# Turning q and k of the last twelve sets by transposing DMA transfers, with scores in tiles of 64 rows and a new order of all engines

## The chip, the core and the metric

The kernel runs on one core of one Trainium2 chip. The metric is device time in microseconds, the median over the executions shown. The engines are TensorE (PE, with its weight loads as PEld), VectorE (DVE), ScalarE (ACT), GpSimd (POOL) and SyncE (SP). PE writes to PSUM, of which the kernel uses eight banks of 128 x 512 f32. DMAs issued by POOL go through queue 0, which can cast f32 to f16 on the way; those issued by SP and ACT go through the hardware queues 1 and 10. All use the core's 16 DMA engines.

## The reference

An attention over 8 batches x 8 heads, 576 tokens, head dimension 64, with 16 "beacon" keys and values ahead of the causal ones, then a two-layer feed-forward net over all 4608 tokens:

```python
k_all = np.concatenate([beacon_k, k], axis=2)          # [8, 8, 592, 64]
v_all = np.concatenate([beacon_v, v], axis=2)
scores = scale * np.matmul(q, k_all.transpose(0, 1, 3, 2))
causal[:, Nb:] = np.triu(np.ones((S, S), dtype=bool), k=1)
scores = np.where(causal, -1000000000.0, scores)
a = np.exp(scores - scores.max(-1, keepdims=True))
a /= a.sum(-1, keepdims=True) + 1e-09
x = (a @ v_all)                                        # [4608, 512] after putting the heads side by side
h = x @ w_in                                           # w_in [512, 2048]
g = h * (1.0 / (1.0 + np.exp(-1.702 * h)))
out = g @ w_out                                        # w_out [2048, 512], out f32
```

## The kernel before

The attention is cut into 16 *sets*: set s is batch s // 2 and four of its eight heads. The work on a set:

- `load_qk` / `e_load_qk` (line 416): POOL issues one casting DMA each for q and k. In the tiles `qn` and `kn` (three buffers each) a head has 32 partitions, and a partition holds a run of 18 tokens (2304 bytes in f16).
- `turns` / `e_turn` (lines 457, 465, 472): DVE casts the beacon keys and turns them, then k and q, by 32x32 transposes on pairs of f16 seen as one f32. In `kT` and `qT` (two buffers each) a head has 32 partitions, one for each pair of its 64 dimensions; the two halves of the pair, d = 0 and 1, lie side by side.
- `chunk` / `e_qk` (line 506): PE makes the scores, keys on partitions, queries on columns. The 1664 columns that the causal mask leaves of a set are cut into chunks of 512 (sets 0 to 3 by a cut of their own); a chunk from set 4 on may end one set and begin the next. Each piece of a chunk is eight matmuls in tiles of 32 rows: for d = 0 and 1, four heads at once, accumulated in PSUM. There are 39 such chunks for sets 4 to 15.
- `e_exp` (line 518) on ACT takes the chunk from PSUM to `E`; `e_mask` (line 536) on POOL zeroes the triangles on the diagonal; DVE adds up key blocks for the sum (`e_zadd`, line 554).
- `e_av` (line 594): PE multiplies `E` by v and by ones, in tiles of 32 columns; DVE turns, inverts and turns the sums (lines 604, 610, 615) and writes the normalised result into `xT` (`e_norm`, line 628), a ring of 2304 token columns.

The feed-forward net works on ten groups of tokens (two of 256, eight of 512). Groups 0 and 1 use plain products (`e_m1`, line 652, and `e_m2`, line 698); groups 2 to 9 make the second product by seven half-size products with sums of blocks (`products`, `e_s` at line 718, `e_prod` at line 770, `e_join` at line 786). Groups 7, 8 and 9 (`FAST`) make the first product that way too (`fast`, `e_part`, line 864), with the sums of weights kept in the buffers of `qn`, `kn` and `bkf` once the sets are done with them.

Nothing is scheduled at run time: `ORDER` at the top is a list of operation numbers for each engine, and `Plan.run` merges the lists into the order in which the program is written, by costs of its own, and hands out PSUM banks: four that any tile of the net and of `e_av` can take, four for scores until the last chunk's exps are done. POOL's DMA issues stand in POOL's list between the masks; the stores, and the small beacon loads, stand in SP's.

PE changes its tile mode between 32-row scores, 32-column value products and full matmuls.

## Time and profile before

| what | us |
|---|---|
| median of 2 runs (320.57 and 320.72) | 320.64 |
| span of the profiled execution | 319.1 |
| PE busy | 312.4 (98%) |
| PE weight loads busy | 223.9 (70%) |
| DVE busy | 246.5 (77%) |
| ACT busy | 220.0 (69%) |
| POOL busy | 113.2 (35%) |
| packets of queue 0, share of 16 DMA engines' span | 49.0% |

The span runs from the first to the last instruction of the profiled execution; the 1.5 us to the median lie around it, and no time of its own is given for that execution besides. Busy times are unions, so a busy PE says that some matmul is in flight and not that the array is filled at its peak. In a line of a view, `out<-in` names what is written and read, with buffer numbers left out; `L506` is line 506 of the kernel before. A wait is put down to what ended it.

### The profile page before, as it was taken

How to read it: one execution, taken by the hardware profiler on the slowest of the kernel's cores; microseconds unless marked ns; L12 is line 12 of the kernel's file. 1: busy time of each engine (PE TensorE's matmuls, PEld its weight loads, DVE VectorE, ACT ScalarE, POOL GpSimd, SP SyncE). 2: the span in 40 equal slices, each digit the busy share in tenths (PEclk: the TensorE clock that was granted, in tenths of full speed). 3: DMA queues.
4: the chain of work that ended last, by engine and by line, in shares of the span. 5: the costliest groups of instructions: out<-in, count | busy, mean ns of one | idle time of the engine just before them, and what ended most of it. 6: DMA issues, size and time to landing. Idle time of an engine off the chain costs nothing.

```text
span 319.1 us, 9554 instructions
## 1 busy us (share of the span) xinstructions
PE 312.4 (98%) x4119; PEld 223.9 (70%) x4119; DVE 246.5 (77%) x484; ACT 220.0 (69%) x275; POOL 113.2 (35%) x178
## 2 busy tenths in 40 slices
PE   6999999999999999999999999999999999999995
PEld 2567855544875467754778877646788888888884
DVE  4769966896797778875788979888978975684773
ACT  1777986557767686698867685778779786666520
POOL 8768488670238413472084108420420000000000
PEclk9999999999999999999999999999999999999999
DMA  7999999993109911398085707710021000011112
GB/s 122 175 202 209 206 192 185 170 228 65 37 2 165 208 26 37 46 153 123 7 81 90 115 2 81 100 35 2 2 83 51 4 20 15 33 69 36 67 68 99
DMA packets 58379, 28.80 MB, mean 90 GB/s; under 512 B 41312, under 2 KB 53728, under 8 KB 58336
## 3 DMA queue, kind: packets, MB, share of 16 engines
q0 software_dynamic: 47552, 18.49, 49.0%
q1 hardware_dynamic: 10576, 9.63, 9.3%
q8 instruction: 32, 0.52, 0.7%
q14 instruction: 11, 0.09, 0.1%
q10 hardware_dynamic: 208, 0.07, 0.1%
HBM read 37.22 MB, written 9.44 MB: 146 GB/s over the span
## 4 chain that ended last, share of the span: by engine, by line
PE 89%; DMA 5%; POOL 2%; ACT 1%; DVE 1%; issue 0%; DVEq 0%; POOLq 0%
PE u L770 31%; PE u L652 25%; PE u L864 12%; PE u L594 9%; PE s L506 8%; PE u L698 5%; DMA kn<-in_k_dram 3%; DMA qn<-in_q_dram 2%; POOL w L438 1%; ACT E L518 1%; ACT L674 0%; DVE kT L472 0%; POOL qn L416 0%; POOL kn L416 0%; ACT g L674 0%
## 5 line engine op out<-in xcount | busy, mean ns | idle before, releaser
L518 ACT ACTIVATE E<-s 128x2048 f16<-128x2048 f32 (+3 forms) x59 | 90.7, 1552 | 35.4 <-PE s L506 32.5
L652 PE MATMUL u<-xT,w 128*128 128x256 f16 (+1 forms) x512 | 87.9, 326 | 0.1
L536 POOL TENSOR_SCALAR_AFFINE_SELECT E<-E 128x512 f16<-128x512 f16 (+3 forms) x78 | 48.7, 643 | 89.6 <-ACT E L518 89.5
L652 PEld LDWEIGHTS <-w 128*128 128x128 f16 x512 | 49.2, 98 | 32.8 <-issue 1.1
L674 ACT ACTIVATE g<-u 128x512 f16<-128x512 f32 x80 | 43.6, 598 | 15.9 <-PE u L652 15.6
L770 PEld LDWEIGHTS <-g 128*128 128x128 f16 x512 | 48.4, 98 | 7.6 <-issue 0.5
L786 DVE SCALAR_TENSOR_TENSOR osb<-u,osb 128x512 f32<-128x512 f32 (+2 forms) x51 | 33.2, 654 | 21.5 <-PE u L770 16.3
L770 PE MATMUL u<-w,g 128*128 128x256 f16 x384 | 49.7, 273 | 0.0
L770 PEld LDWEIGHTS <-sA 128*128 128x128 f16 x384 | 36.6, 98 | 6.0 <-issue 0.8
L892 ACT ACTIVATE g<-u 128x512 f16<-128x512 f32 x48 | 27.2, 602 | 14.0 <-PE u L864 8.6
L506 PEld LDWEIGHTS <-kT 32*128 32x128 f16 x1088 | 22.4, 92 | 17.5 <-issue 10.8
L770 PE MATMUL u<-tB,sA 128*128 128x256 f16 x256 | 34.2, 273 | 0.0
L628 DVE TENSOR_TENSOR xT<-u,rz 128x352 f16<-128x352 f32 (+2 forms) x52 | 26.1, 521 | 8.4 <-PE u L594 7.7
L506 PE MATMUL s<-qT,kT 32*128 32x192 f16 (+14 forms) x992 | 30.9, 247 | 0.5 <-ACT E L518 0.3
L432 POOL DMA_DIRECT2D vb<-in_v_dram x32 | 27.8, 873 | 3.1 <-PE u L594 1.4
L594 PE MATMUL u<-E,vb 128*32 128x352 f16 (+8 forms) x928 | 27.7, 262 | 0.1
L594 PEld LDWEIGHTS <-vb 128*32 128x32 f16 (+1 forms) x928 | 20.1, 96 | 6.7 <-issue 2.9
L554 DVE TENSOR_TENSOR zs<-zs,E 128x1344 f16<-128x1344 f16 (+2 forms) x36 | 21.8, 605 | 0.9
L472 DVE STREAM_TRANSPOSE kT<-kn 128x576 f32<-128x576 f32 x16 | 20.1, 1256 | 2.7 <-DMA kn<-in_k_dram 2.2
L718 DVE TENSOR_TENSOR sA<-g 128x512 f16<-128x512 f16 x32 | 13.2, 417 | 10.9 <-ACT g L674 10.7
L472 DVE STREAM_TRANSPOSE qT<-qn 128x576 f32<-128x576 f32 x16 | 19.8, 1240 | 0.8 <-DMA qn<-in_q_dram 0.7
L864 PEld LDWEIGHTS <-w 128*128 128x128 f16 x192 | 18.7, 98 | 2.3
(76 smaller groups left out, 401.1 us busy)
## 6 DMA issues: line engine op xcount, KB each, us to landing
out_dram<-osb SPq DMA_DIRECT2D x35, 256.0 KB, 2.6
kn<-in_k_dram POOLq DMA_DIRECT2D x16, 288.0 KB, 6.8
qn<-in_q_dram POOLq DMA_DIRECT2D x16, 288.0 KB, 6.4
vb<-in_v_dram POOLq DMA_DIRECT2D x24, 128.0 KB, 6.8
w<-in_moe_w_in_dram POOLq DMA_DIRECT2D x8, 256.0 KB, 9.4
w<-in_moe_w_out_dram POOLq DMA_DIRECT2D x4, 512.0 KB, 12.1
vb<-in_v_dram POOLq DMA_DIRECT2D x8, 112.0 KB, 6.0
vb<-in_v_dram POOLq DMA_DIRECT2D x8, 80.0 KB, 6.8
```

What stands on the lines that cost most here:

```text
L432: nc.gpsimd.dma_start(out=t[0 : hi - lo, j, h0:h1, :], in_=v[b, h0:h1, lo:hi, :].rearrange("h n d -> n h d"),)
L472: nc.vector.transpose(out=f32(dst.rearrange("p n e -> p (n e)")).rearrange("p (r t) -> p t r", t=TR), in_=f32(src[:, :]).rearrange("p (t c ...
L506: nc.tensor.matmul(u[:, o : o + w], kT[s % NB2][r : r + 32, j * P : (j + 1) * P, d], qT[s % NB2][r : r + 32, a : a + w, d], start=(d == 0) ...
L518: nc.scalar.activation(out=Es[s][:, h0:h1, c0:c1], in_=sall[(i, p)][:, :, o : o + c1 - c0], func=AFT.Exp, scale=0.125,)
L536: nc.gpsimd.affine_select(out=blk, in_=blk, compare_op=ALU.is_ge, fill=0.0, base=off + (Nb if j == 0 else 0), pattern=[[0, Q], [1, w]], ch ...
L594: nc.tensor.matmul(u[32 * h : 32 * h + 32, a:e], lhs, src[0:kw, h, col : col + e - a], start=first, stop=last, skip_group_check=s >= EARLY ...
L652: nc.tensor.matmul(u[:, o + a - t0 : o + e - t0], w1t[:, kp, nt * P : (nt + 1) * P], xT[:, kp, a % XR : (e - 1) % XR + 1], start=(kp == 0 ...
L674: nc.scalar.activation(out=gts[g][:, n0:n1, 0:w], in_=rings[("m1", g, n0)][:, 0 : n * w].rearrange("p (n w) -> p n w", n=n), func=AFT.Gelu ...
L770: nc.tensor.matmul(u[:, HM * mt : HM * (mt + 1)], lhs[:, n, mt * P : (mt + 1) * P], rhs[:, n, :], start=(n == 0 and (mt == 0 or apart) and ...
L786: nc.vector.scalar_tensor_tensor(out=osbs[(g, dst)][:, c0:c1], in0=rings[("p", g, p)][:, c0:c1], scalar=scale_of(g), in1=osbs[(g, src)][:, ...
L864: nc.tensor.matmul(u[:, HM * n : HM * (n + 1)], lhs[x][:, (2 * i + n) * P : (2 * i + n + 1) * P], rhs[:, x, :], start=fresh and n == 0 and ...
L892: nc.scalar.activation(out=gts[g][:, n : n + 2, HM * h : HM * (h + 1)], in_=rings[src][:, :].rearrange("p (n w) -> p n w", n=2), func=AFT. ...
```

## The change

- Sets 0 to 3 are turned as before, from two buffers instead of three. For sets 4 to 15, q and k of a whole batch (two sets) are first loaded into `qS` and `kS`, tokens on partitions and all eight heads side by side: per batch five loads of q, five of k and one of the beacon keys, all issued by POOL (`e_stage`). `qS` and `kS` have one buffer each, whose memory is also that of the early sets' `qn` and `kn`; the loads of a batch wait until the batch before it is turned.
- SP then issues ten transposing DMAs a set (`e_xbar`), five for k and five for q, each of up to 128 tokens x 256 columns (four heads), into the memory of `kT` and `qT`, now seen as `kP` and `qP`: two heads on 128 partitions, 64 dimensions each, and two such pairs behind one another. They wait for the scores of the set two earlier.
- The scores of these sets take four matmuls a piece in tiles of 64 rows, one a head, with no accumulation.
- `xT` becomes a ring of 2048 columns, so that a group never crosses its end, but a set's normalising can; it is then cut in two.
- The block sums of the second product are made in place in `g`, except the first (`sA` shrinks from three tiles to one); the second then waits for product 1, the third for product 2. The sums of weights and the saved product of `fast` get tiles of their own (`SF`, `x7`).
- `ORDER` is new for all engines, and `BANK` gives the PSUM bank of every tile. The numbers of operations changed, so a line-by-line difference of the lists says nothing. Listed engine by engine, PE goes from 4119 recorded matmuls, 768 of them scores of sets 4 to 15, to 384 such; its changes of tile mode go from 148 to 142. In PE's order the first scores of set 4 come after 13 of the 16 quarters of groups 0 and 1's second product, where they came after three of them.

```diff
@@ -300,18 +333,28 @@
     ones = cst.tile([P, 64], F16, tag="ones", name="ones")
     w1t = cst.tile([P, NKT, DFF], F16, tag="w1", name="w1")
     w2t = cst.tile([P, NNT, DMODEL], F16, tag="w2", name="w2")
-    XR = 4 * S
+    XR = 2048
     NPL, NPE, GEL = 2, 10, 2
     HM, HN = 256, NNT // 2
     xT = cst.tile([P, NKT, XR], F16, tag="xT", name="xT")
-    sA = [cst.tile([P, HN, HM], F16, tag=f"sA{i}", name=f"sA{i}") for i in range(3)]
+    sA = cst.tile([P, HN, HM], F16, tag="sA", name="sA")
+    SF = {i: cst.tile([P, 2, DFF // 2], F16, tag=f"SF{i}", name=f"SF{i}") for i in (1, 2, 4)}
+    NX7 = 2
+    x7 = [cst.tile([P, 512], F32, tag=f"x7{i}", name=f"x7{i}") for i in range(NX7)]
     tB = [cst.tile([P, HN, HM], F16, tag=f"tB{i}", name=f"tB{i}") for i in range(3)]
-    bkf = cst.tile([P, NSET, D], F32, tag="bkf", name="bkf")
+    SQR = 2 * HS
+    bkf = cst.tile([P, SQR, D], F32, tag="bkf", name="bkf")
     bkn = cst.tile([P, 2, D], F16, tag="bkn", name="bkn")
-    qn = [cst.tile([P, TR * D], F16, tag=f"qn{i}", name=f"qn{i}") for i in range(NB3)]
-    kn = [cst.tile([P, TR * D], F16, tag=f"kn{i}", name=f"kn{i}") for i in range(NB3)]
-    qT = [cst.tile([P, S, 2], F16, tag=f"qT{i}", name=f"qT{i}") for i in range(NB2)]
-    kT = [cst.tile([P, NKPAD, 2], F16, tag=f"kT{i}", name=f"kT{i}") for i in range(NB2)]
+    qS = cst.tile([P, NJ, H * D], F16, tag="qS", name="qS")
+    kS = cst.tile([P, NJ, H * D], F16, tag="kS", name="kS")
+    qn, kn = (
+        [x[:, :, :].rearrange("p j c -> p (j c)")[:, i * TR * D : (i + 1) * TR * D] for i in range(NB3)]
+        for x in (qS, kS)
+    )
+    qTt = [cst.tile([P, 2 * S], F16, tag=f"qT{i}", name=f"qT{i}") for i in range(NB2)]
+    kTt = [cst.tile([P, 2 * NKPAD], F16, tag=f"kT{i}", name=f"kT{i}") for i in range(NB2)]
+    qT, kT = ([t[:, :].rearrange("p (n e) -> p n e", e=2) for t in x] for x in (qTt, kTt))
+    qP, kP = ([t[:, :].rearrange("p (c n) -> p c n", c=2) for t in x] for x in (qTt, kTt))
     vb = [cst.tile([P, NJ, H, D], F16, tag=f"vb{i}", name=f"vb{i}") for i in range(NB2)]
 
     zt = cst.tile([P, HF], F32, tag="zt", name="zt")
...
@@ -434,6 +477,32 @@
                 in_=v[b, h0:h1, lo:hi, :].rearrange("h n d -> n h d"),
             )
 
+    def span(which, j):
+        lo = j * P - (Nb if which else 0)
+        return max(0, lo), min(lo + P, S)
+
+    def e_stage(b, which, j):
+        t = (qS, kS)[which]
+        if j < 0:
+            nc.gpsimd.dma_start(
+                out=t[0:Nb, 0, :].rearrange("p (h d) -> p h d", h=H), in_=beacon_k[b].rearrange("h n d -> n h d")
+            )
+            return
+        lo, hi = span(which, j)
+        p0 = Nb if which and j == 0 else 0
+        nc.gpsimd.dma_start(
+            out=t[p0 : p0 + hi - lo, j, :].rearrange("p (h d) -> p h d", h=H),
+            in_=(q, k)[which][b, :, lo:hi, :].rearrange("h n d -> n h d"),
+        )
+
+    def e_xbar(s, which, j):
+        src, dst = ((qS, qP), (kS, kP))[which]
+        rows = P if which else min(P, S - j * P)
+        c = Q * D * (s % HS)
+        nc.sync.dma_start_transpose(
+            out=dst[s % NB2][:, :, j * P : j * P + rows], in_=src[0:rows, j, c : c + Q * D],
+        )
+
     def e_load_w1(hs, c0, c1):
         nc.gpsimd.dma_start(
             out=w1t[:, 2 * hs : 2 * hs + 2, c0:c1],
...
@@ -500,6 +569,17 @@
             if s not in Es:
                 Es[s] = ep.tile([P, Q, ETOT], F16, tag="E", name="E")
         for (w, s, j, a, o) in qk_pieces(i):
+            if s >= SQR:
+                for h, u in heads.items():
+                    r = D * (h % 2)
+                    nc.tensor.matmul(
+                        u[:, o : o + w],
+                        kP[s % NB2][r : r + D, h // 2, j * P : (j + 1) * P],
+                        qP[s % NB2][r : r + D, h // 2, a : a + w],
+                        start=True,
+                        stop=True,
+                    )
+                continue
             for d in range(2):
                 for h, u in heads.items():
                     r = 32 * h
...
@@ -625,12 +705,16 @@
         t0 = (b * S + a) % XR
         rz = zs[(s, half)] if s < EARLY else zs[(s, 0)][:, a:e]
         n = 2 if s >= EARLY and half == 0 else 1
-        nc.vector.tensor_tensor(
-            out=xT[:, 2 * hs + x : 2 * hs + x + n, t0 : t0 + w],
-            in0=rings[("av", s, x, half)][:, 0 : n * w].rearrange("p (n w) -> p n w", n=n),
-            in1=rz[:, 0:w].rearrange("p (o w) -> p o w", o=1).to_broadcast([P, n, w]),
-            op=ALU.mult,
-        )
+        cut = min(w, XR - t0)
+        for c0, c1 in ((0, cut), (cut, w)):
+            if c0 < c1:
+                at = (t0 + c0) % XR
+                nc.vector.tensor_tensor(
+                    out=xT[:, 2 * hs + x : 2 * hs + x + n, at : at + c1 - c0],
+                    in0=rings[("av", s, x, half)][:, 0 : n * w].rearrange("p (n w) -> p n w", n=n)[:, :, c0:c1],
+                    in1=rz[:, c0:c1].rearrange("p (o w) -> p o w", o=1).to_broadcast([P, n, c1 - c0]),
+                    op=ALU.mult,
+                )
 
     GROUPS = [(0, 256), (256, 512)]
     while GROUPS[-1][1] < NTOK:
...
@@ -740,13 +824,13 @@
 
     def e_s(g, i, n0, n1, eng):
         a11, a12, a21, a22 = (quarter(g, x, y)[:, n0:n1, :] for x in range(2) for y in range(2))
-        s1, s2, s4 = (t[:, n0:n1, :] for t in sA)
+        s1 = sA[:, n0:n1, :]
         if i == 0:
             add(eng, s1, a21, a22, ALU.add)
         elif i == 1:
-            add(eng, s2, s1, a11, ALU.subtract)
+            add(eng, a11, s1, a11, ALU.subtract)
         elif i == 2:
-            add(eng, s4, a12, s2, ALU.subtract)
+            add(eng, a12, a12, a11, ALU.subtract)
         else:
             add(eng, a21, a11, a21, ALU.subtract)
 
...
@@ -756,10 +840,10 @@
         lhs, rhs = {
             1: (quarter(g, 0, 0), w(0, 0)),
             2: (quarter(g, 0, 1), w(1, 0)),
-            3: (sA[2], w(1, 1)),
+            3: (quarter(g, 0, 1), w(1, 1)),
             4: (quarter(g, 1, 1), tb(2)),
-            5: (sA[0], tb(0)),
-            6: (sA[1], tb(1)),
+            5: (sA, tb(0)),
+            6: (quarter(g, 0, 0), tb(1)),
             7: (quarter(g, 1, 0), tb(3)),
         }[p]
         apart = g == NG - 1 and p in (3, 5)
...
-    PHASE = {}
-    plan.breaks = sorted(set(PHASE.values())) + [len(CHUNKS) - 1]
-    SF, ST = {}, {}
-
-    def pair(a, b):
-        return [t[:, 0 : DFF // 2] for t in (a, b)]
-
-    SF[1], SF[2] = pair(qn[1], kn[1]), pair(qn[2], kn[2])
-    SF[4] = bkf[:, :, :].rearrange("p a d -> p (a d)").bitcast(F16).rearrange("p (x n) -> p x n", x=2)
-    SF[4] = [SF[4][:, x, :] for x in range(2)]
...
-        if slot is None:
-            p7s[(g, i)] = os.tile([P, DMODEL], F32, tag="osb", name="osb")[:, :]
-        else:
-            p7s[(g, i)] = f32((qn[0], kn[0])[slot][:, 0 : 2 * 512])
+        p7s[(g, i)] = x7[slot][:, :] if slot < NX7 else f32((qn[0], kn[0])[slot - NX7][:, 0 : 2 * 512])
         nc.scalar.mul(out=p7s[(g, i)], in_=rings[src][:, :], mul=1.0)
 
     def e_sum7(g, i, src, dst):
...
+    staged, padded = {}, []
+
     def load_batch(b):
-        for s in range(HS * b, HS * b + HS):
-            for which in (1, 0):
-                load_qk(s, which, max(0, due_of(s) - 22000))
+        if not padded:
+            padded.append(op(
+                "DVE", 150, [turn[(s, 1)] for s in range(SQR)], lambda: nc.vector.memset(kS[64:P, NJ - 1, :], 0.0),
+                name="padk",
+            ))
+        for which in (1, 0):
+            for j in range(-which, NJ):
+                deps = [turn.get((s, which, jj)) for s in range(HS * b - HS, HS * b) for jj in range(NJ)]
+                deps += padded if which else [turn[(s, 0)] for s in range(SQR)]
+                staged[(b, which, j)] = pool_load(
+                    870 if j >= 0 else 560, 900 if j >= 0 else 200, deps, lambda which=which, j=j: e_stage(b, which, j),
+                    name=f"ldqk{2 * b}",
+                )
         for j in range(-1, NJ):
             load_v(b, j, max(0, due_of(HS * b) - 12000))
 
...
@@ -949,6 +1038,15 @@
         ]
 
     def turns(s):
+        if s >= SQR:
+            b = s // HS
+            for which in (1, 0):
+                for j in range(NJ):
+                    turn[(s, which, j)] = op(
+                        "SP", XBAR, [staged.get((b, which, x)) for x in ((j, -1) if j == 0 else (j,))]
+                        + [qks[i] for i in CH_OF.get(s - NB2, [])], lambda which=which, j=j: e_xbar(s, which, j), name=f"xbar{s}",
+                    )
+            return
         urgent = s < HS
         cast = op(
             "DVE", 180, ld_bk[s] + [turn.get((s - 2, 1))], lambda: e_bk(s),
...
-    tds, ends = {}, {}
+    tds, ends, fives = {}, {}, {}
 
     def products(g):
-        eng = "POOL" if g < SDVE else "DVE"
+        eng = "DVE"
         sd = {}
-        for n0 in range(0, HN, SQ):
-            n1 = n0 + SQ
-            prev = []
-            for i in range(4):
-                deps = prev + done.get(g - 1, [])
-                for n in range(n0, n1):
-                    deps += gates[(g, n)] + gates[(g, n + HN)]
-                d = 336
-                o = op(eng, d, deps, lambda n0=n0, n1=n1, i=i: e_s(g, i, n0, n1, eng), pr=2, name=f"s{g}")
-                prev = [o]
+
+        def sums(i, deps):
+            for n0 in range(0, HN, SQ):
+                n1 = n0 + SQ
+                o = op(
+                    eng, 336, deps(n0) + [x for n in range(n0, n1) for x in gates[(g, n)] + gates[(g, n + HN)]],
+                    lambda n0=n0, n1=n1: e_s(g, i, n0, n1, eng), pr=2, name=f"s{g}.{i}.{n0}",
+                )
                 sd[(i, n0)] = o
+
+        sums(0, lambda n0: fives.get(g - 1, []))
+        sums(3, lambda n0: [sd[(0, n0)]])
         lhs = {1: None, 2: None, 3: 2, 4: None, 5: 0, 6: 1, 7: 3}
+        made = {}
         rhs = {1: None, 2: None, 3: None, 4: 2, 5: 0, 6: 1, 7: 3}
         last = {}
 
...
+            if p == 1:
+                sums(1, lambda n0: [sd[(3, n0)], made[(1, n0)]])
+            elif p == 2:
+                sums(2, lambda n0: [sd[(1, n0)], made[(2, n0)]])
+            elif p == 5:
+                fives[g] = [prev[0]]
 
         def join(p, src, dst, deps=(), closes=True, at=None):
             return op(
...
         ph = plan.breaks.index(PHASE.get(g, len(CHUNKS) - 1))
         if not wsum:
-            both = lambda s: [turn[(s, 0)], turn[(s, 1)]]
-            free = {
-                1: both(NSET - 3), 2: both(NSET - 2), 4: [bkc[NSET - 1]],
-                3: [x for n in range(g) for x in m1s[n]],
-            }
+            free = {3: [x for n in range(g) for x in m1s[n]]}
+            loads = [x for n in w1_of for x in w1_of[n]]
             prev = None
             for i in (1, 2, 4, 3):
-                prev = wsum[i] = op("DVE", 1250, free[i] + [prev], lambda i=i: e_ws(i), name="wsum")
-        free = readers.get(g - 1, [])
+                prev = wsum[i] = op("DVE", 1250, free.get(i, []) + loads + [prev], lambda i=i: e_ws(i), name="wsum")
+        free = readers.get(g - 1, list(gated))
         xsum, prev = {}, None
         for i in (1, 2, 4, 3):
             prev = xsum[i] = op("DVE", 336, free + xs + [prev], lambda i=i: e_xs(g, i), name=f"xsum{g}")
+            m1s.setdefault(g, []).append(prev)
         lhs = {3: 4, 5: 1, 6: 2, 7: 3}
-        fixed = g not in PHASE
 
         def tiles(i):
```

`BANK`, the lists of `ORDER`, the waiting times that `Plan.lat` assumes for stores and for the transposes, and some bookkeeping of dependencies are left out.

More of the change, by code (lines that the diff above doesn't have):

```diff
@@ L180, in opening @@
                 if None not in ends:
-                    open_at.append((max([0] + [x + 60 for x in ends]), i))
+                    open_at.append((max([since] + [x + 60 for x in ends]), key not in self.partial, i))
             return min(open_at, default=None)
@@ L1064, in values @@
             else:
+                split = 65 if (b * S + q0) // XR != (b * S + q1 - 1) // XR else 0
                 norms[(s, half, x)] = op(
-                    "DVE", 65 + 1.045 * cols * (2 if whole and half == 0 else 1), [avs[(s, x, half)], z2[0 if whole else half]],
+                    "DVE", 65 + split + 1.045 * cols * (2 if whole and half == 0 else 1), [avs[(s, x, half)], z2[0 if whole else half]],
                     lambda x=x, half=half: e_norm(s, x, half),
@@ L1242, in tiles @@
             k = len(held)
[L1243 to L1246 removed]
+            slot = k % (NX7 if g < LATE else NX7 + 2)
+            last = used.get(slot, [x for y, x in turn.items() if y[0] >= NSET - HS] if slot >= NX7 else [])
             def part(p, at, deps, fresh=False):
[L1249 removed]
+                deps = list(deps) + xs
                 if p in lhs:
@@ L1385 @@
                 values(s)
-                while s % HS == HS - 1 and g < FAST[0] and GROUPS[g][1] <= (s // HS + 1) * S:
+                while s % HS == HS - 1 and g < NG and GROUPS[g][1] <= (s // HS + 1) * S:
                     mlp(g)
                     g += 1
-    for g in FAST:
-        mlp(g)
     def also(o, d):
```

57 lines of the change are left out of this document (36 added, 21 removed), and 179 rows, old and new, of tables (BANK, ORDER).

## The prediction

> **What bounds the kernel now.** I read first the busy time by stretches (the windows), which says which engine is full and when; then who waited for whom; then the timeline around score chunks, to price one; then the groups and DMA issues that the change removes or resembles.
>
> ```profile
> core 0: us, PE busy (x) PEld busy (x) DVE busy (x) ACT busy (x) POOL busy (x), PEclk, DMA share, GB/s
> ...
> 8.50:20.00 11.50, 11.48 (x214) 7.02 (x213) 8.43 (x23) 9.52 (x11) 7.88 (x15) 1.00 1.56 184
> 20.00:46.00 26.00, 25.45 (x453) 18.89 (x452) 21.36 (x40) 22.55 (x26) 18.00 (x30) 1.00 1.34 201
> 46.00:120.00 74.00, 73.91 (x936) 43.45 (x935) 57.83 (x109) 51.77 (x61) 35.68 (x56) 1.00 0.90 122
> 120.00:235.00 115.00, 115.00 (x1656) 80.96 (x1654) 96.07 (x181) 85.30 (x91) 42.69 (x63) 1.00 0.45 63
> 235.00:315.70 80.70, 80.61 (x858) 71.16 (x856) 58.05 (x121) 49.59 (x89) 1.78 (x4) 1.00 0.13 45
> ```
> From 46 to 315.7 us PE is idle for 0.18 us of 269.7, while DVE is idle for 57.8. Before 20 us PE's time is mostly warm-up matmuls (line 1416) between scores; there ACT is the full engine (9.5 of 11.5 us).
>
> ```profile
> POOL E L536 <- ACT E L518: 89.5, 29, 13.3
> ACT E L518 <- PE s L506: 32.5, 33, 2.3
> ...
> PE u L1416 <- DVE tB L327: 2.6, 1, 2.6
> ...
> PE s L506 <- ACT E L518: 0.3, 1, 0.3
> PE s L506 <- DVE kT L472: 0.2, 1, 0.2
> ```
> The last three are all that PE waited for. ACT waits for PE's scores, and POOL for ACT. The DVE transposes cost PE one wait of 0.2 us.
>
> A busy PE need not be at its peak, so I price it by starts:
>
> ```profile
> 94.29 0.65 PE L506 MATMUL s<-qT,kT 32*128 32x208 f16 x32
> 94.86 1.04 PE L594 MATMUL u<-E,vb 128*32 128x224 f16 x36
> ...
> 126.14 1.05 PE L770 MATMUL u<-w,g 128*128 128x256 f16 x8
> 127.12 0.64 PE L506 MATMUL s<-qT,kT 32*128 32x384 f16 x24
> 127.69 0.48 PE L594 MATMUL u<-E,vb 128*32 128x352 f16 x8
> ...
> 184.42 0.63 PE L506 MATMUL s<-qT,kT 32*128 32x512 f16 x8
> 184.98 0.38 PE L594 MATMUL u<-zs,ones 128*32 128x288 f16 x8
> ```
> A chunk of 512 score columns holds PE from its start to the next one's: 0.57, 0.57 and 0.56 us for 32, 24 and 8 matmuls. The clock is granted whole (1.00), and a 256-wide full matmul starts every 0.109 us, or 0.42 ns a column. Two passes (d = 0, 1) of 512 columns, four heads at once, are then 0.43 us; 0.13 to 0.14 is the way in and out of the tile mode. Ahead of it, eight full matmuls take 0.98 us (126.14 to 127.12) where 8 x 0.109 is 0.87: 0.1 for a change of mode.
>
> ```profile
> L432 POOL DMA_DIRECT2D vb<-in_v_dram x32 | 27.8, 873 | 3.1 <-PE u L594 1.4 <-DMA w<-in_moe_w_out_dram 0.7 <-DMA qn<-in_q_dram 0.5
> ...
> L472 DVE STREAM_TRANSPOSE kT<-kn 128x576 f32<-128x576 f32 x16 | 20.1, 1256 | 2.7 <-DMA kn<-in_k_dram 2.2
> ...
> L472 DVE STREAM_TRANSPOSE qT<-qn 128x576 f32<-128x576 f32 x16 | 19.8, 1240 | 0.8 <-DMA qn<-in_q_dram 0.7
> ...
> L416 POOL DMA_DIRECT2D kn<-in_k_dram x16 | 9.2, 575 | 9.0 <-DVE kT L472 3.8 <-DVE bkn L457 2.6 <-DVE zt L604 0.8
> ```
>
> In these group lines the last figures before the idle time are busy us and mean ns of one. Only 2.9 us of DVE's idle time ahead of the transposes is a wait for their loads.
>
> **The change part by part**, against the profiled execution: 319.1 us of span, and 1.5 us around it to the median of 320.64.
>
> DVE. Twelve sets lose two transposes (1.256 and 1.240), a cast (0.243) and a small transpose (0.193): 12 x 2.93 = 35.2 us of 246.5 busy. Six more normalising pieces and one memset come back, below 3 us at the 0.5 of such rows. On the path: PE's whole wait for these transposes was 0.2 us, so I take 0, bounds 0 and -0.2. What stands behind them is PE's own work.
>
> PE, scores. 39 chunks go from 32-row to 64-row tiles: half as many matmuls (768 to 384), each over the whole head dimension, two heads at once where there were four. Columns: 2 x 512 either way, 0.43 us. Fewer instructions: 0.57 less 0.56 over 24 matmuls is about 0.6 ns each, 384 x 0.6 = 0.2 us gained. No row shows a 64-row tile. Bounds: the 32-row rows, where tiles overlap fully (-0.2), and full matmuls, which don't: four times 512 columns at 0.42 ns, 0.43 us more a chunk, 39 x 0.43 = +16.8. I take -0.2, as the row-tiled rows are the nearest.
>
> PE, the rest. The ring of xT has 2048 columns, a multiple of a group, so no group of line 652 is cut: 128 narrow matmuls fewer, 64 of 512 more; 128 x 0.1093 - 64 x 0.2157 = 0.2 gained. The instruction listings of the two kernels have 148 and 142 changes of tile mode in PE's order: 6 x 0.1 = 0.6 gained. The product matmuls (lines 770 and 864) keep their number and width.
>
> POOL and queue 0. Per batch, four loads (0.57 each) become ten of v's shape (0.87) and one small (0.55): 9.3 us of POOL for 2.3, six times, +42 us on 113. Cover: the 89.5 us for which POOL waited for ACT. Without cover, up to 7 us a batch would fall on the masks behind them. On the queue, v loads issued one behind the other at 42 to 55 us land 0.5 to 0.85 us apart and the q and k loads 1.4; so a batch asks 8.7 us where it asked 5.6, out of some 33 (sets 8 and 12 begin at 118.82 and 184.42, two batches apart). The share was 1.34 and 0.90 of 16 engines early on, 0.45 later. I take 0; the bounds are 0 and the 42.
>
> SP. 120 transposes, 20 a batch, stand in one queue with the stores, and a set's ten wait for the scores of the set two earlier. A store behind a waiting transpose waits too, and its buffer with it. No row has a transpose. Nearest: plain issues on SP, 0.31 to 0.82 us each (bkf, median 0.42), landing 1.6 to 7.7 us later (stores, median 2.3). At 0.42 a set needs 10 x 0.42 + 2.3 = 6.5 us; at 0.82, 10.5. The new order leaves, summed at the PE prices above, 21, 10.5, 23, 25, 13.6, 17.5, 25, 26, 11.9 and 19 us of PE work between the release and first use of sets 6 to 15. All fit, so 0. If each ran alone, at the 1.6 of the fastest landing and 2.3 at the end, a set needs 18.3: late by 7.8 (set 7), 4.7 (10), 0.8 (11) and 6.4 (14), +20 us. Bounds 0 and +20; I take 0, since SP's issues are seen 0.42 apart without waiting for landings.
>
> [...]
>
> Products. The sums of line 718 are now made in place, so the second waits for product 1 to have read its block and the third for product 2. The next product follows PE's own 16 matmuls (1.7 us) later, and a sum takes 0.42: covered while other work stands between. In the last group I allow 0 to +1.
>
> Sets 4 and 5 share their staging memory with the early sets' loads, so their 10 loads wait for set 3's turn. The order therefore puts their scores behind 39.6 us of PE work (31.2 before), filled with the products of the first groups. Those products wait for second weights, which are now issued between staged loads. Bounds: 0, and +4 if a load there lands as late as the slowest v load did (13.7 us, not some 9). I take 0.
>
> ACT gets two more table loads (2 x 1.28), beside its 30 idle us of 120 to 235.
>
> Sum: -0.2 - 0.2 - 0.6 = -1.0; 320.6 - 1.0 = **319.6 us**.
>
> **The rivals.**
> *The transposes are late* (slower). For: one queue, and 20 a batch with stores between. Against: SP's plain issues at 0.42. It decides where a set needs over about 14 us, that is near 1.15 us a transpose with 2.3 at the end: sets 7 and 14 are then late by 3.3 and 1.9, set 10 by 0.2, together 5 to 6 us, near the 2% that a measurement of this kernel can tell from no change. At 1.6 it gives 320.6 - 1.0 + 20 = 340 us. Chance 0.18.
> *64-row tiles take turns.* 319.6 + 16.8 = 336 us. For: nothing but the lack of a row. Chance 0.04.
> [...] Chance 0.03. [...]
> *The start shortens.* To 46.09 us, where 31.2 us of real PE work are done after scores began at 8.56, 6.3 us are lost. Were all regained: 313.3. Against: ACT is the full engine there (9.52 of 11.5, 22.55 of 26) and keeps its work. Chance 0.05.
>
> **How the numbers follow.** Forecast 0.70 (own range 317.5 to 323: the start may give 2, the last group and the first staging cost up to 4). Faster by over 2%: 0.07 (instructions, start). Slower: 0.22 (late transposes, tiles in turn). The remaining 0.71 is within 2%. The range is 316 to 332: it leaves out about 0.06 below and 0.12 above, transposes slower than 1.35 us among it.
>
> **What would show it.** Right: from 50 to 310 us PE is as full as now, score chunks of 4 to 16 matmuls take 0.55 to 0.57 us, DVE has some 213 us busy, POOL 155, and no PE wait names qT or kT. Wrong: PE waits for a transfer into qT or kT, first of all before sets 7, 14 and 10; chunks near 1 us; masks late behind loads; or scores of set 4 later than about 55 us with PE idle.

## The result, and the profile after

The changed kernel takes 371.9 us (370.94 and 372.87) against 320.64: 1.160 times as long, with a 95% interval of 1.153 to 1.167. The forecast was 319.6, with a range of 316 to 332. The profiled execution took 370.94 us, with a span of 368.6.

The busy time in the first four of the stretches shown for the kernel before:

```profile
core 0: us, PE busy (x) PEld busy (x) DVE busy (x) ACT busy (x) POOL busy (x), PEclk, DMA share, GB/s
8.50:20.00 11.50, 10.75 (x206) 6.47 (x207) 9.51 (x24) 8.37 (x10) 7.19 (x12) 1.00 1.58 182
20.00:46.00 26.00, 25.25 (x473) 19.02 (x462) 19.95 (x36) 23.87 (x27) 20.20 (x32) 1.00 1.49 162
46.00:120.00 74.00, 61.47 (x703) 36.28 (x701) 35.13 (x66) 38.55 (x40) 45.60 (x58) 0.95 1.36 120
120.00:235.00 115.00, 92.36 (x884) 55.54 (x883) 55.31 (x113) 65.77 (x77) 53.15 (x74) 0.88 0.97 103
```

PE, which was idle for 0.18 us from 46 us on, is now idle for 12.5 us of the third stretch and 22.6 us of the fourth, and there the granted clock is 0.95 and 0.88. No engine took PE's place as the full one: DVE and ACT are idle for about half of these two stretches. Something that is no engine's work is late. The waits name it (in each line: who waited, for whom, us, times, longest):

```profile
ACT E L598 <- PE s L575: 61.5, 29, 12.1
POOL E L616 <- ACT E L598: 57.8, 15, 14.4
DVE zs L634 <- POOL E L616: 33.9, 9, 8.4
PEld L575 <- issue: 31.2, 29, 11.1
...
POOL qS L493 <- DMA qT<-qS: 17.1, 3, 7.8
PE s L575 <- DMA qT<-qS: 16.6, 2, 10.9
...
POOL kS L493 <- DMA kT<-kS: 14.5, 3, 7.8
```

Line 575 is the scores in 64-row tiles, 493 the staging loads, 502 the transposes. PE waits for a transposing DMA, ACT for PE, POOL for ACT, DVE for POOL: the whole chain stands. And POOL's loads wait for transposes in their turn. What SP does at one such stop, from the timeline around set 8:

```profile
134.61 0.58 SPq L878 DMA_DIRECT2D out_dram<-osb  x1
...
135.29 1.17 SPq L502 DMA_TRANSPOSE qT<-qS  x1
...
135.56 0.22 PE L674 MATMUL u<-E,ones 128*32 128x112 f16 x4
...
136.50 2.53 SPq L502 DMA_TRANSPOSE kT<-kS  x2
139.14 2.48 SPq L502 DMA_TRANSPOSE qT<-qS  x2
141.16 0.90 POOL L493 DMA_DIRECT2D kS<-in_k_dram  x1 [16.77 <-issue]
141.67 0.57 SPq L878 DMA_DIRECT2D out_dram<-osb  x1
...
142.29 5.04 SPq L502 DMA_TRANSPOSE qT<-qS  x4
...
146.71 0.61 PE L575 MATMUL s<-qT,kT 64*128 64x512 f16 x2 [10.93 <-DMA qT<-qS]
```

SP is hardly ever idle here: it works off transposes at 1.2 us each while PE stands still for 10.9 us. At another stop it is the masks that are late. POOL, from 191 us on:

```profile
191.07 0.69 POOL L493 DMA_DIRECT2D qS<-in_q_dram  x1 [4.69 <-DMA qT<-qS]
191.76 0.60 POOL L616 TENSOR_SCALAR_AFFINE_SELECT E<-E 128x448 f16<-128x448 f16 x1
192.30 1.78 POOL L493 DMA_DIRECT2D qS<-in_q_dram  x2
194.05 0.56 POOL L487 DMA_DIRECT2D kS<-in_beacon_k_dram  x1
194.59 0.67 POOL L616 TENSOR_SCALAR_AFFINE_SELECT E<-E 128x512 f16<-128x512 f16 x1
```

A load waits 4.7 us for the transposes that still read `qS`; the masks stand behind it, and DVE behind the mask:

```profile
195.30 1.55 DVE L634 TENSOR_TENSOR zs<-E 128x1856 f16<-128x1856 f16 x1 [6.12 <-POOL E L616]
196.77 0.41 DVE L802 TENSOR_TENSOR g<-g 128x512 f16<-128x512 f16 x1
197.10 0.68 DVE L870 SCALAR_TENSOR_TENSOR osb<-u,osb 128x512 f32<-128x512 f32 x1
```

PE, whose next product needs the bank that the last of these lines empties, goes on at 197.84 after 4.5 us. All 120, by line 502 (ns, shortest, median and longest), and their landing:

```profile
L502 SPq DMA_TRANSPOSE qT<-qS x60: 1159/1222/2507, 39.1 to 267.9; - x60
L502 SPq DMA_TRANSPOSE kT<-kS x60: 1168/1198/2067, 45.7 to 269.2; - x60
...
DMA to landing us min/median/max: 2.3/3.6/8.8
```

Where one starts within 2.7 us of the last (106 times), the starts are 1.29 us apart in the median and 1.46 on average, stores between them included. A batch of two sets is 20 of them, some 29 us, and the kernel before spent 32.8 us on a batch. In the changed kernel the first transposes of one batch and of the next are 40.4 us apart on average.

Each of the four longest stops is followed, or overlapped, by a stretch at half clock:

```profile
106.90:113.70 6.80, 3.64 (x52) 2.19 (x55) 0.53 (x1) 1.94 (x2) 2.78 (x4) 0.50 0.36 35
141.10:151.30 10.20, 4.59 (x22) 2.74 (x23) 1.36 (x3) 1.88 (x1) 5.56 (x8) 0.50 0.89 97
195.70:202.50 6.80, 4.67 (x26) 2.79 (x26) 4.47 (x7) 0.08 (x1) 6.80 (x10) 0.50 1.59 134
223.00:233.20 10.20, 5.33 (x48) 3.23 (x49) 3.52 (x9) 3.58 (x3) 3.06 (x4) 0.50 1.10 130
sum 34.00, PE 18.22 PEld 10.94 DVE 9.88 ACT 7.48 POOL 18.20; mean PE 4.56 PEld 2.74 DVE 2.47 ACT 1.87 POOL 4.55
```

Four matmuls of 256 columns take 0.83 us from start to start there (from 147.68 us on) and 0.44 at full clock. PE works 18.2 us at half clock, so by that, as an estimate, 9.1 us are lost on top of the idle time. In the changed kernel these stretches, of 6.8 and 10.2 us, lie around stops of PE of 4.5 to 10.9 us; its stops of 1.9 to 2.2 us (at 57.0, 67.7 and 252.6 us) had none, nor had the kernel before (clock 1.00 throughout). In the runs below stops of some 3 us went either way: one of 2.5 us in `e_both` (mean clock 0.983) was followed by 3.4 us at half clock, one of 3.1 us in `e_turns_out` (mean clock 1.00) by none. So a stop of 2.5 us was not always safe.

To see where the time went, I follow PE's own work: the matmuls in their order, each priced at its columns' share of the 0.109 us of a 256-wide full matmul (tiles that lie side by side share it). The table says how many us later than in the kernel before PE reaches a given sum of work, in the changed kernel and in some of the experiments below (in the order of the columns `e_all_out`, `e_turns_out`, `e_third_sorted_loads_out` and `e_both`).

| work done, us | before, at | changed | all transposes out | those of sets 6 to 15 out | third buffer, sorted, loads out | all buffers |
|---|---|---|---|---|---|---|
| 0.1 (first scores) | 8.7 | +1.7 | +1.9 | +1.7 | +1.6 | +2.0 |
| 20 | 38.7 | +1.1 | +2.7 | +1.6 | +2.3 | +3.1 |
| 60 | 81.2 | +6.9 | +3.2 | +9.0 | +9.4 | +8.7 |
| 80 | 103.8 | +16.3 | +5.3 | +11.1 | +11.5 | +10.9 |
| 100 | 124.7 | +29.4 | +5.2 | +11.0 | +11.4 | +10.8 |
| 120 | 146.5 | +29.5 | +5.3 | +11.1 | +11.5 | +12.5 |
| 140 | 168.1 | +36.2 | +5.6 | +11.4 | +11.7 | +12.7 |
| 160 | 188.9 | +45.7 | +5.5 | +11.4 | +11.7 | +12.7 |
| 180 | 210.6 | +48.0 | +6.0 | +11.8 | +12.1 | +21.7 |
| 280 | 312.5 | +49.3 | +7.2 | +13.1 | +13.4 | +23.0 |

The changed kernel loses its time in steps: before sets 4 and 5 (to 60), at sets 7 (80) and 8 (100), to 140 at the product that waits for DVE (above), and before sets 12 (160) and 14 (180).

### The profile page after: what moved, and what is told of

It reads as the page before. It is cut to its first block, busy times and chain, and to the rows that moved or that the text cites. A ratio compares the mean times of both kernels' runs of the same rounds, so it can differ in the third digit from the quotient of the medians.

```text
span 368.6 us, 8852 instructions
## 1 busy us (share of the span) xinstructions
PE 322.4 (87%) x3667; PEld 222.0 (60%) x3667; DVE 218.4 (59%) x441; ACT 222.9 (60%) x277; POOL 154.3 (42%) x220
## 4 chain that ended last, share of the span: by engine, by line
PE 57%; SPq 15%; DMA 12%; DVE 4%; POOL 4%; ACT 4%; issue 3%; DVEq 0%; POOLq 0%; ACTq 0%
PE u L854 23%; SPq L502 14%; PE u L736 12%; PE u L943 10%; PE u L674 5%; PE s L575 5%; DMA qT<-qS 4%; ACT E L598 3%; DMA w<-in_moe_w_out_dram 2%; DMA kT<-kS 2%; DMA bkf<-in_beacon_k_dram 2%; DMA out_dram<-osb 2%; DVE g L802 2%; POOL qS L493 1%; PE p L586 1%
## 5 line engine op out<-in xcount | busy, mean ns | idle before, releaser
L736 PE MATMUL u<-xT,w 128*128 128x512 f16 (+1 forms) x448 | 87.9, 349 | 0.6 <-ACT g L758 0.3
L854 PEld LDWEIGHTS <-g 128*128 128x128 f16 x768 | 75.2, 101 | 16.1 <-issue 3.4
L854 PE MATMUL u<-w,g 128*128 128x256 f16 x512 | 69.9, 281 | 0.1
L736 PEld LDWEIGHTS <-w 128*128 128x128 f16 x448 | 42.8, 98 | 39.0 <-issue 2.3
L758 ACT ACTIVATE g<-u 128x512 f16<-128x512 f32 x80 | 44.2, 599 | 13.7 <-PE u L736 13.1
L575 PE MATMUL s<-qT,kT 64*128 64x80 f16 (+22 forms) x384 | 25.7, 261 | 30.3 <-DMA qT<-qS 16.6
L493 POOL DMA_DIRECT2D qS<-in_q_dram x30 | 25.7, 866 | 32.1 <-DMA qT<-qS 17.1
L493 POOL DMA_DIRECT2D kS<-in_k_dram x30 | 25.7, 867 | 31.7 <-issue 17.2
L854 PE MATMUL u<-tB,g 128*128 128x256 f16 x256 | 38.1, 283 | 0.8 <-DVE xT L712 0.7
L968 ACT ACTIVATE g<-u 128x512 f16<-128x512 f32 x48 | 26.8, 598 | 15.0 <-PE u L943 11.7
L712 DVE TENSOR_TENSOR xT<-u,rz 128x352 f16<-128x352 f32 (+6 forms) x58 | 26.2, 481 | 13.9 <-PE u L674 13.2
L802 DVE TENSOR_TENSOR g<-g 128x512 f16<-128x512 f16 x64 | 27.7, 451 | 0.2
L634 DVE TENSOR_TENSOR zs<-E 128x1856 f16<-128x1856 f16 x12 | 14.4, 1201 | 16.3 <-POOL E L616 16.3
```

Source lines behind the costliest of these rows:

```text
L493: nc.gpsimd.dma_start(out=t[p0 : p0 + hi - lo, j, :].rearrange("p (h d) -> p h d", h=H), in_=(q, k)[which][b, :, lo:hi, :].rearrange("h n ...
L575: nc.tensor.matmul(u[:, o : o + w], kP[s % NB2][r : r + D, h // 2, j * P : (j + 1) * P], qP[s % NB2][r : r + D, h // 2, a : a + w], start= ...
L634: nc.vector.tensor_tensor(out=t, in0=E[:, :, Z0:S] if i == 1 else t, in1=E[:, :, wcol[i] : wcol[i] + S - a], op=ALU.add,)
L736: nc.tensor.matmul(u[:, o + a - t0 : o + e - t0], w1t[:, kp, nt * P : (nt + 1) * P], xT[:, kp, a % XR : (e - 1) % XR + 1], start=(kp == 0 ...
L758: nc.scalar.activation(out=gts[g][:, n0:n1, 0:w], in_=rings[("m1", g, n0)][:, 0 : n * w].rearrange("p (n w) -> p n w", n=n), func=AFT.Gelu ...
L802: (nc.vector if eng == "DVE" else nc.gpsimd).tensor_tensor(out=out, in0=a, in1=b, op=op)
```

## The experiments

Each time below is one run; the kernel before took 320.5 to 321.3 us on the same chips. The two runs of the changed kernel are 1.9 us apart, so differences below some 2 us say nothing. The theory (A): SP pays about 1.25 us for each transposing DMA, and with the release of the two turned buffers and the single staging buffer around them they come late. Rivals: the staging loads themselves (B), the new order or the sums in place (C).

**1. Without the transposes.** `e_turns_out` has the first of these edits, `e_turns_loads_out` both:

```diff
     def e_xbar(s, which, j):
+        if s >= 6:
+            return
...
     def e_stage(b, which, j):
+        if b >= 3:
+            return
```

> The changed kernel with the transposing DMAs of sets 6 to 15 left out (100 of 120; the scores of those sets read what sets 4 and 5 left in qT and kT). Everything else, the staging loads on POOL too, is issued as in the changed kernel. Theory A, the transposes are the cause (1.25 us of SP each, in line, between a release and a need, with the loads behind them): back to 316 to 323 us, no half clock behind set 6. Rival B, the staging loads and POOL's issue of them hold PE up: 345 us or more. Rival C, the new order of the engines and the sums in place cost by themselves: 345 us or more here and in the next run.

> The changed kernel with the transposing DMAs of sets 6 to 15 and also the staging loads of q and k of batches 3 to 7 left out (stale data in the scores). A: the same as with the transposes alone left out, within 3 us (316 to 323). B: clearly below that run, 316 to 323 where that one was 345 or more. C: still 345 or more.

Measured: 333.8 and 335.4 us. The transposes of sets 6 to 15 cost 371.9 - 333.8 = 38 us, and the loads that are left in the first run cost nothing that can be told (1.6 us the other way): B falls, since its loads run there. But it is not 316 to 323: 13 us stay, which neither A nor any rival had as a number. PE's waits in the first of them:

```profile
PE s L577 <- DMA kT<-kS: 4.7, 2, 3.1
PE u L1522 <- DVE tB L370: 2.6, 1, 2.6
PE u L784 <- DMA w<-in_moe_w_out_dram: 1.7, 2, 1.2
PE u L856 <- DVE xT L714: 0.8, 1, 0.8
```

The first is sets 4 and 5, whose transposes are still there.

**2. Without any transpose, and without any load.** The same edits with a bare `return`.

> The changed kernel with all 120 transposing DMAs left out, those of sets 4 and 5 too (stale data in the scores of sets 4 to 15), the staging loads kept. The run without those of sets 6 to 15 took 333.8 us and its TensorE still stood still for 2.0 us before set 4 and 3.3 us before set 5. If these two waits are all that the first transposes cost: 327 to 330 us. If the first transposes cost nothing beyond and the new order and the sums in place are what is left over before: 332 us or more. If all of it is the transposes: 319 to 323.

> The changed kernel without any of the 120 transposes and without any staging load of q and k (sets 4 to 15 score stale data). Without the transposes alone it took 328.7 us, 8 above the kernel before. If the staging loads, on POOL and queue 0, make that: 321 to 325 us. If it is the new order of the engines itself: 327 to 330.

Measured: 328.7 and 328.5 us. So the first 20 transposes cost 5 us, and 8 us remain that are neither transposes nor loads. That leaves the new order, the sums in place or the early sets' two buffers. The table shows them as small waits, +1.9 at the first scores and then a little everywhere. Ahead of the first scores DVE's cast of the beacon keys waits 5.2 us for a DMA into `bkf` (0.85 in the kernel before), and PE waits 1.9 us for the cast. This part of C stands; which of the three makes the 8 us was not separated.

**3. Loads out, transposes kept; and half the columns.** `e_loads_out` has only the second edit of 1; `e_half_turns` cuts each DMA:

```diff
-            out=dst[s % NB2][:, :, j * P : j * P + rows], in_=src[0:rows, j, c : c + Q * D],
+            out=dst[s % NB2][:, 0:1, j * P : j * P + rows], in_=src[0:rows, j, c : c + P],
```

> The changed kernel with the staging loads of q and k of batches 3 to 7 left out, all 120 transposes kept (they turn the data of batch 2 again). If the chain turn, load, turn on the single staging buffer is what makes the transposes late: 318 to 328 us, transposes running ahead as soon as their buffer is released. If SP's 1.25 us each between release and need is enough by itself: 335 to 365. B: 316 to 325.

> The changed kernel with each transposing DMA cut to 128 of its 256 columns (two heads of four are turned, the other two are stale); the count of 120 stays. If SP's time is per instruction: 1.2 us each again and 365 to 373 us. If it is per block of data: 0.6 to 0.7 us each, SP's need falls to half, and 322 to 340 us.

Measured: 358.8 and 368.4 us. Without loads 13 us are gained and 25 (358.8 - 333.8) stay. The time lies in the range for release to need alone (335 to 365): the reload is a part of the cause, and release to need the larger. With half the columns 3.5 us are gained, as expected for a price for each instruction, and the lines say why:

```profile
L502 SPq DMA_TRANSPOSE qT<-qS x60: 1090/1182/2268, 40.6 to 266.1; - x60
L502 SPq DMA_TRANSPOSE kT<-kS x60: 1093/1186/2117, 46.2 to 267.3; - x60
```

1.18 us for half the data where it was 1.20 to 1.22: SP pays for the DMA, and hardly for its size.

**4. Five blocks in one DMA.** Staging is laid out by set, so that a set's five blocks of k lie side by side and are turned together; the scores of k read that order.

```diff
-    kS = cst.tile([P, NJ, H * D], F16, tag="kS", name="kS")
+    kS = cst.tile([P, HS, NJ, Q * D], F16, tag="kS", name="kS")
...
+        n = NJ if which else 1
+        if j < n - 1:
+            return
...
+            out = dst[s % NB2][:, 0 : 2 * P * n].rearrange("p (b r) -> p b r", r=P)
```

> The run without staging loads for batches 3 to 7 took 358.8 us, with 20 transposes in a batch of two sets. Here, besides, the five blocks of k of a set are turned by one DMA (128 x 1280 into ten blocks), so that SP issues 12 in a batch and not 20; loads of batch 2 in halves of four heads. Stale data in the scores of sets 6 to 15. Theory A, revised: SP pays 1.2 us for each transposing DMA, whatever its size (half the columns took 1.18 us): 12 of 1.3 us are 16 us in 33 us, and 330 to 342 us. Rival: SP pays for the blocks, some 6 us for such a DMA: 353 to 362.

> The changed kernel with the five blocks of k of a set turned by one DMA, its scores reading k in that order; staging loads in halves of four heads, 22 instead of 11 in a batch. Nothing is left out. Theory A, revised, with a price for each DMA: the loop of 12 transposes (17 us), reload (10 to 12 us) is 29 us, below the 33 us of a batch: 332 to 348 us. With a price for each block: 365 us or more.

Measured: 345.2 and 352.2 us, 3 and 4 us above the ranges for a price for each DMA, and 8 and 13 below those for a price for each block. The DMA itself, in the second kernel:

```profile
L514 SPq DMA_TRANSPOSE qT<-qS x60: 1159/1198/2302, 40.3 to 244.6; - x60
L514 SPq DMA_TRANSPOSE kT<-kS x12: 1254/1412/2857, 49.3 to 242.6; - x12
```

Five times the data for 0.21 us more. The fastest landings are 2.28 us for 64 KB (in the changed kernel) and 2.96 for 320 KB: 256 KB more in 0.68 us, by which the rate is, as an estimate, 385 GB/s. What put them above the expectation is probably the start: with loads in halves, PE has a first stop of 6.9 and 5.9 us near 50 us, inside the plain products of the first groups (`e_m2`). In the second kernel PE waits 7.0 us there for second weights, whose loads stand behind those of q and k in POOL's list.

**5. The order of SP's list, and a third pair of turned buffers.** Sorting (`e_sorted`); the buffers besides, in tiles that the net needs only later (`e_third_sorted`); and the staging loads of batches 3 to 7 left out as well:

```diff
+        at = [n for n, o in enumerate(todo["SP"]) if o.name[:4] == "xbar"]
+        for n, o in zip(at, sorted((todo["SP"][n] for n in at), key=lambda o: o.name, reverse=True)):
+            todo["SP"][n] = o
...
+    qTt.append(SF[2][:, :, :].rearrange("p x n -> p (x n)")[:, 0 : 2 * S])
+    kTt.append(SF[1][:, :, :].rearrange("p x n -> p (x n)")[:, 0 : 2 * NKPAD])
+    at = [(s - 4) % 3 if 4 <= s < 12 else s % 2 for s in range(NSET)]
```

> The changed kernel with the 120 transposes sorted by set, then block, over the same places of SP's list (in the list as it is, sets s and s+1 are mixed, and a later set's transposes stand ahead of an earlier one's). If waits in the list (a transpose that waits for its buffer ahead of one that could go) are a large part: 345 to 360 us. If the chain of staging and release sets the time: 365 to 373.

> The sorted list, and a third pair of turned buffers for sets 6 and 9 (in tiles that the fast multiplication needs only later), so that sets 4 to 11 turn over three buffers and a set's transposes need only the scores of three sets earlier to be done; sets 12 to 15 have two as before. If release to need is the window that is too short: 335 to 352 us, and no wait of TensorE over 2 us for sets 7 to 11. If the rate of SP itself, 20 of 1.29 us and the stores in 33 us, or the loads behind the turns set it: 355 us or more.

> The sorted list with the third pair of turned buffers (sets 6 and 9), and the staging loads of batches 3 to 7 left out (stale data). Each alone left 372.1 and 358.8 us. Theory A, revised: two chains hold the transposes, release to need, and reload behind the last transpose of a batch; with both cut, SP has 29 us of work in 33: 330 to 345 us, with waits left only at sets 4, 5 and 12 to 15. Rival: SP's rate alone is too low: 352 us or more.

Measured: 374.3, 372.1 and 334.4 us. Neither the sorting nor the third pair gives anything while the loads are chained to the transposes. The longest stop of `e_third_sorted` is 15.1 us and no wait for `qT` or `kT`: PE waits for DVE, DVE 15.7 us for a mask, and ahead of that mask in POOL's list stand staging loads that wait for transposes. With both chains cut, the 100 transposes of sets 6 to 15, at the same price, cost 0.6 us against the run without them (334.4 - 333.8), or nothing against the one without their loads too (335.4). This is the run that decides: SP's rate is not the bound, and the price of a transpose matters here only through what it is chained to. The first transposes of two batches are 32.8 us apart here on average, the pace of the kernel before. Of PE's waits one is left that belongs to a transpose:

```profile
PE s L584 <- issue: 3.0, 1, 3.0
PE u L1529 <- DVE tB L377: 2.6, 1, 2.6
PE u L791 <- DMA w<-in_moe_w_out_dram: 1.7, 2, 0.9
PE u L745 <- issue: 1.1, 1, 1.1
```

The 3.0 us stand ahead of the first scores of set 4. The view names no releaser, but they end 0.2 us after the landing of the fourth block of q, which these scores need. From set 6 on PE waits for no transpose.

**6. Two queues.**

```diff
-        nc.sync.dma_start_transpose(
+        (nc.sync if which else nc.scalar).dma_start_transpose(
```

> The changed kernel with the 60 transposes of q issued by ScalarE instead of SP, at the places that the plan gives them (those of k stay on SP). If the 1.25 us belong to the issuing queue: SP is busy with 75 us instead of 150, ScalarE with 75 us more, and the time falls to 340 to 360 us, with the exponentials later. If the transposes share one unit for the whole core, each takes longer when both queues issue (2 us and more), and the time stays at 365 us or rises.

Measured: 477.8 us. It rises, as the second expectation allowed, but not for its reason, since a transpose takes no longer: the price is the same on ACT (median 1.19 us), as the first had it. The waits show what else happened:

```profile
POOL E L616 <- ACT E L598: 147.4, 24, 28.2
DVE sA L802 <- ACT g L758: 112.6, 10, 29.6
PEld L736 <- issue: 103.3, 114, 13.6
PE u L736 <- ACT g L758: 70.6, 14, 13.3
```

Exponentials and gelus stand behind waiting transposes in ACT's list, and PE, DVE and POOL behind them. Moreover the two queues did not transpose at the same time in this run: the 120 change queue 37 times, and not once did one start before the last of the other queue has landed. What an overlap would give was not tried.

**7. The buffers with nothing left out.** `e_stage2` has a second staging buffer for batches 3 and 5 in `SF` tiles. `e_both` has the sorted list and the third pair besides. In `e_early` (sorted list, no third pair) and `e_both_early` POOL's staging loads of batches 4 to 7 are moved ahead, two in front of each mask:

```diff
+    ALT, SFT = (3, 5), dict(SF)
+    def staging(b, which, j):
+        if b not in ALT:
+            return (qS, kS)[which][:, j, :]
...
+        pool = todo["POOL"][::-1]
+        for b in range(4, 8):
+            mine = [o for o in pool if o.name == f"ldqk{2 * b}" and o.lands is not None]
...
+                pool[n:n] = mine[:2]
```

> The changed kernel with a second staging buffer for batches 3 and 5 (in tiles that the fast multiplication needs only later), so that the loads of batches 3 to 6 no longer wait for the transposes of the batch before; nothing is left out. Theory A, revised: as the run without those loads (358.8) or a little above: 356 to 364 us, and POOL's waits for transposes nearly gone. Rival: the loads take transfer time from the transposes, not order: 368 us or more.

> Nothing left out: the sorted list, the third pair of turned buffers (sets 6 and 9) and the second staging buffer (batches 3 and 5) together; POOL's list as in the changed kernel. Theory A (buffers alone tie the transposes: release to need, and reload): 334 to 345 us. Theory D (POOL's list ties them: a staging load stands behind masks there, masks wait for the exponentials and these for the scores, so that late scores make late loads, whatever the buffers): 355 to 372.

> Nothing left out: the sorted list, the second staging buffer, and POOL's staging loads of batches 4 to 7 moved ahead in its list, two in front of each mask from the set before the last one of the batch before on; two turned buffers as in the changed kernel. A: as the run with the second staging buffer (373.2): 366 to 374. D: the loads are in time, the release is left: as the run without these loads (358.8), 353 to 364.

> Nothing left out: all four, the sorted list, the third pair of turned buffers, the second staging buffer and the loads ahead in POOL's list. A and D: both chains are cut for batches 4 to 6, and what is left is the start of sets 4 to 6, the last batch, where buffers are single again, and masks behind the loads: 334 to 346 us, without a wait of TensorE above 3 us between 110 and 200 us. If a price of the transposes was overlooked: 352 or more.

Measured: 373.2, 344.4, 353.3 and 351.1 us. The second staging buffer alone does nothing, against my expectation: POOL's waits for transposes are nearly gone there (4.5 + 4.0 us), but its list still has loads behind masks, which wait for late scores (102.4 us of waiting for ACT). The time lies in the range of the rival, that the loads take transfer time; but `e_both` has all the same loads. With the loads moved ahead (`e_early`) 20 us come back against `e_stage2`, D's number. With both buffers and POOL's list as it was (`e_both`), 29 us: theory A's number, at its upper end, so with scores in time POOL's list does little harm. Both together (`e_both_early`) miss what both theories gave, and are worse than the buffers alone: loads in front of masks make the masks late (DVE waits 22.6 us for them, 13.2 in `e_both`, and PE 7.8 us for DVE's sums behind them, 0.4 in `e_both`). What `e_both` still pays is in the table: 9 us before set 14, in the last batch, which has neither a second staging buffer nor a third pair, and for the rest the loss of the run without transposes from set 6 on. PE's waits there:

```profile
PE s L598 <- DMA qT<-qS: 8.5, 2, 6.0
PE u L1547 <- DVE tB L380: 2.6, 1, 2.6
PE p L609 <- DVE bkn L549: 1.7, 1, 1.7
PE u L759 <- issue: 1.6, 1, 1.6
```

With this order no version of the transposes beat the kernel before, and none was likely to: without any of them it takes 328.7 us.

## Why the prediction was wrong, point by point

*What bounds the kernel, DVE, POOL, ACT.* The reading of the profile before holds, and so nearly do the busy times: DVE fell to 218.4 (213 forecast), POOL rose to 154.3 (155). DVE's 28 us bought nothing that shows, as forecast: PE's whole wait for its transposes of q and k had been 0.2 us.

*Scores in 64-row tiles.* Right. A chunk holds PE for 0.54 to 0.56 us from its start to the next one's, at full clock:

```profile
85.63 0.61 PE L575 MATMUL s<-qT,kT 64*128 64x320 f16 x8
86.17 1.92 PE L854 MATMUL u<-w,g 128*128 128x256 f16 x16
```

In turns a chunk would take 0.43 us more, so these tiles overlap fully; the rival "64-row tiles take turns" is out. The forecast gives a chance of 0.03 to a gain from fewer instructions; no run shows its term, and what the runs show is a chunk of 0.546 us on average at full clock where it was 0.569, by which the 384 matmuls fewer saved some 0.9 us in 39 chunks.

*The transposes on SP.* This is the step that failed: "Bounds 0 and +20; I take 0, since SP's issues are seen 0.42 apart without waiting for landings." A transposing DMA holds SP for 1.2 us, at half the size too, three times the row that I took as nearest, and the starts are 1.46 us apart on average. The rival "the transposes are late" had part of the mechanism, and its point of decision, 1.15 us a transpose, was passed. It named sets 7, 10 and 14; stops came at 7, 8, 12 and 14. But it too was too small. Its own sum at 1.25 us a transpose gives 14.8 us a set and +4.3, +1.2 and +2.9 for sets 7, 10 and 14, about +8 us; the runs have 38, so the upper bound of +20 failed too. The windows from release to first use were counted as if each set stood alone. What the runs put in the place of that is a loop. The transposes waited for loads that waited for the batch before to be turned (13 us of it goes with the loads, `e_loads_out`). The loads stood in POOL's list behind masks that wait for late scores (20 us, `e_early` against `e_stage2`; `e_early` has the sorted list too, which alone gained nothing). And PE's clock fell to half at the long stops (9 us). These shares overlap and do not add up to 38. In SP's list, besides, a set's transposes stood among those of the next, but sorting them alone gained nothing (374.3).

*POOL and queue 0.* "I take 0" is right for the loads by themselves: with the transposes gone they cost nothing that can be told (333.8 with them, 335.4 without). The cover named, POOL's waiting for ACT, was there. What was overlooked is that the loads and the transposes wait for each other.

*Start, sets 4 and 5.* 0 to +4, taken as 0. Measured 5 us (333.8 - 328.7) for these 20 transposes. PE's waits in experiment 1 put 4.7 us of it to transposes of k and 1.7 to second weights: mostly the same price, and less what the step named, a late load of weights.

*PE, the rest, and the products.* -0.2 - 0.6 and 0 to +1. The 1.0 us of the whole sum does not show: without any transpose PE is busy for 312.4 us, as in the kernel before, and its idle time grows by 8 (328.7 us). That the new order would be as tight as the old one was taken for granted in every term, and no view of the kernel before could show it.

*The rate of the transposes.* By the 256 KB more in 0.68 us of experiment 4, as an estimate, the 64 KB of one transpose take 0.17 us, where SP is held for 1.20 to 1.22. The price of the issue was what I lacked, and what else waits for it.

## What to carry to other kernels

The price of an instruction that no trace shows is not that of its nearest relative: give it a range of several times, and look where the time goes at each end, through every loop that it is part of (buffer released, loaded, turned, used), not one window at a time. A chain of transfers that takes 29 of 33 us cost 0.6 us here when nothing in it waited for what it feeds (`e_third_sorted_loads_out`), and 38 when it did; one buffer more at each of two stages, with a sorted list, bought back 28 of the 38 us, and each of the two buffers without the other bought nothing. When work moves from an engine with slack to a queue, count what the queue pays per instruction first, and merge instructions (five blocks in one DMA cost 1.41 us where five DMAs cost 6).

## What the runs showed of the hardware

A transposing DMA within SBUF held SP for 1.18 us at 128 x 128 (`e_half_turns`), 1.20 to 1.22 at 128 x 256 (the changed kernel) and 1.41 at 128 x 1280 (`e_merge_k`), all medians, and ScalarE for 1.19 at 128 x 256 (`e_two_queues`). Those of 64 KB landed 2.28 us after their issue at the earliest (the changed kernel), those of 320 KB 2.96 us (experiment 4). PE's half clock lasted 6.8 to 10.2 us around stops of 4.5 to 10.9 us in the changed kernel, and 3.4 us after stops of 2.5 us in `e_both` and 3.0 us in `e_third_sorted_loads_out`; after one of 3.1 us in `e_turns_out` there was none.
